# The third group of tokens joins the groups that are worked in seven products of halves

## The chip, the cores and the metric

The kernel runs on one core of a Trainium2 chip. Its engines are TensorE (PE, matrix products into PSUM banks), VectorE (DVE) and ScalarE (ACT), which work on SBUF and PSUM, GpSimd (POOL) and SyncE (SP), which here issues most transfers. Each engine takes its own instructions strictly in the order in which the program lists them, and waits at the first whose inputs or buffers are not ready. The metric is the device time of one execution in microseconds.

## The reference

```python
a = phi - np.max(phi, axis=2, keepdims=True)     # over the sequence
a = np.exp(a); a = a / (np.sum(a, axis=2, keepdims=True) + 1e-09)
k_m = np.einsum('bhsm,bhsd->bhmd', a, k)         # 32 memory slots per head
v_m = np.einsum('bhsm,bhsd->bhmd', a, v)
scores = 1.0 / np.sqrt(64) * np.matmul(q, k_m.transpose(0, 1, 3, 2))
attn = np.exp(scores - np.max(scores, axis=-1, keepdims=True))
attn = attn / (np.sum(attn, axis=-1, keepdims=True) + 1e-09)
x = np.matmul(attn, v_m).transpose(0, 2, 1, 3).reshape(4608, 512)
h = x @ w_in                                     # 512 x 2048
out = np.maximum(0.01 * h, h) @ w_out            # 2048 x 512
```

There are 8 batches of 576 tokens and 8 heads of 64 columns; all data are float32. Each batch's attention (steps a0 to a7) is followed by two dense products over all 4608 tokens.

## The kernel before

The heads' outputs are never formed. For each batch b the 256 rows of slot values are multiplied with w_in first, a "fold" in four quarters j (steps W{b}{j}): `.p` is the products on TensorE (L1241) into two PSUM banks `pa`, `.h0/.h1` ScalarE's high float16 halves of them (L1274), `.l0/.l1` VectorE's low halves (L1280). The pool of `pa` banks holds three, and the attention and the next fold use the same ones, so that a fold's products wait until the halves of the fold before have been taken. The folded quarter is then the weight of the first dense product, and the attention weights are its input. In float16 each product is three products: high by high, high by low, low by high.

The tokens are worked in groups. Groups 0 and 1 have 384 tokens (GT), group 2 had 256 (GL). These three go the old way: 8 units a group, each with two up-products (P, L1342, or u...P in the first group), the leaky step on ScalarE (V, L1349), a high half (C, L1361, ScalarE), a low half (L, L1365, VectorE) and the down-products (O, L1413) of 512 columns, for each 128 tokens and f tile three. The finished rows leave by Z (L1400).

The 4608 − 1024 other tokens are 14 late groups of 256 tokens and 512 inner columns at a time ("quarters", k = 4 per group). They go by seven products of halves in place of eight: up-products p (L1454), the leaky step v (L1468 and L1470), sums and differences of the four halves s (VectorE, L1484 to L1486), high halves c (ScalarE, L1490, 768 and 1024 columns), low halves l (VectorE, L1494, the same), and the seven down-products d (L1517), each 6 matmuls of 256 columns. Once for each group, x combines the results (L1527 on ScalarE, L1530 to L1537 on VectorE), and z scales and sends them (L1541). The very last group has steps of its own (end, L1564).

The order on all engines is written out by hand, as two lists of steps that run() calls in turn, OPENING (321 steps) and LATER (1846 steps): a step issues all its instructions, on whatever engines, at its place. The transfers stand in it too: i0 to i3 and o0 to o3 load and unpack the quarters of w_in and w_out (ld issues the transfers on SyncE, L389 and L393; y, t, h unpack them on VectorE and ScalarE, L405, L423, L403, L414; i3 is the last quarter of w_in). The slot sums of a batch are a{b}.C10 (L793), the reduction over its slots a{b}.A1 (L655), the transposing of scores L1119.

One SBUF tile, `arena`, holds what changes owner over time. The late groups' scratch lies where the loads and the old groups' halves lay before; `w_mem` holds batch 0's weights and then folded weights.

Of the kernel before, what the change touches and what calls it, by code (L numbers as in the profile page):

```python
# [52 lines left out]
a1.kv0 u3.V0 o2.h2 o2.h1 a1.A1 u2.O0 u3.V1 a1.A2 a1.A3 u4.P1 a1.B0 a1.kv2 a1.kv3 o2.t1 i1.b o2.y2
u4.P0 a1.B10 a1.B20 a1.B3 u3.O0 u4.V0 a1.C10 u5.P1 a1.C2 a1.q1 o2.t2 a1.q0 a1.C30 o0.b a1.C31 i3.ld1
u2.O1 a1.C4 i3.ld0 a1.Q1 o1.b a1.C3k i3.ld2 a1.D11 a1.D2 o2.b a1.D5 a1.D4 a1.D10 a1.D3 a1.Q0 i3.h0
u5.V1 u3.O1 o3.ld2 i3.h1 a1.E1 i3.y1 i2.b u4.V1 i3.t1 a1.E21 o3.ld1 i3.y2 i3.h2 i3.y0 i3.t2 a1.E20
i3.t0 u5.P0 u5.V0 u4.O0 o3.y2 o3.h2 i3.b u5.O0 a1.E22 f03.1 o3.t2 ci.1 o3.y1 a0.S18 u4.O1 a1.S01
a1.S11 ci.2 o3.h1 o3.ld0 a1.S02 a1.S03 ci.3 a1.S12 a1.S04 o3.t1 o3.y0 a2.phi f03.2 ci.4 o3.h0 e.
# [37 lines left out]
a3.D4 v2.2 Z2.1 W23.l0 p3.1 a3.Q1 a3.D5 a3.D6 d0.5 a4.A3 v3.1 d0.4 s2 p3.0 p3.3 c2.0 a4.B10 a3.E1
l2.0 v3.3 v3.0 d0.6 a3.E21 a3.E22 c2.1 p3.2 d1.2 d2.0 l2.1 p4.1 W30.p a4.B20 v3.2 d1.1 W30.h0 d1.4
v4.1 d2.2 p4.3 a3.E20 p4.0 s3 c3.0 W30.h1 l3.0 a3.E23 d1.6 c3.1 a4.kv d1.3 v4.0 W30.l0 p4.2 d2.1
v4.3 a3.S01 l3.1 W31.p d2.3 p5.1 W31.h0 d3.0 v4.2 a3.S02 v5.1 W31.h1 d2.4 os3 a4.B3 d1.5 p5.0 a3.S03
# [1631 lines left out]
```

## Time and profile before

| | us |
|---|---|
| runs | 640.47, 639.00, 640.07 (median 640.07) |
| the profiled execution | 639.66 |
| its span, first to last instruction | 637.9 |
| TensorE busy | 629.6 |
| VectorE busy | 518.1 |
| ScalarE busy | 402.0 |
| GpSimd busy | 12.5 |

The span is what the trace covers; 1.76 us of the execution lie around it. Busy times of matmuls are modelled and overlap in the lists, so that the sum over matmuls is more than the time they take up; spacings between their starts are not. The clock granted to TensorE was 0.999 of full speed over the run. All rows of the trace on which the prediction rests stand in a section of their own below.

### The profile page before, as it was taken

What the parts mean: (1) busy time and instruction counts of PE and PEld (TensorE: products, weight loads), DVE (VectorE), ACT (ScalarE), POOL (GpSimd) and SP (SyncE); (2) the same over time, 40 slices, a digit from 0 to 9 for tenths busy, and PEclk for the clock granted to TensorE, in tenths of its full rate; (3) what the DMA queues carried; (4) which work ended last, traced back from release to release, by engine and by line L of the source; (5) the groups of instructions that cost most, each with busy time, mean ns of one, the idle gap of its engine ahead of it and who ended that gap; (6) DMA issues with size and microseconds to landing.
All of it is one profiled execution on the core that took longest, in us unless ns stands there. A gap on an engine that the chain in (4) does not pass through costs nothing.

```text
span 637.9 us, 17249 instructions
## 1 busy us (share of the span) xinstructions
PE 629.6 (99%) x7365; PEld 490.0 (77%) x7365; DVE 518.1 (81%) x825; ACT 402.0 (63%) x698; POOL 12.5 (2%) x34
## 2 busy tenths in 40 slices
PE   8999999999999999999999999999999999999997
PEld 4545446666577788888888888888888989898886
DVE  5776799999889998898977788899788787755573
ACT  3898998967746665574555655655555656554560
POOL 0000120100000000000000000000000000000000
PEclk9999999999999999999999999999999999999999
DMA  9999821362334434414300504305041100010021
GB/s 326 351 392 271 274 83 25 102 113 75 117 74 83 166 54 95 150 42 65 84 10 17 165 19 93 72 10 183 2 76 35 35 1 17 19 34 2 4 61 37
DMA packets 85404, 61.16 MB, mean 96 GB/s; under 512 B 61648, under 2 KB 68560, under 8 KB 85328
## 3 DMA queue, kind: packets, MB, share of 16 engines
q1 hardware_dynamic: 84752, 59.51, 33.1%
q8 instruction: 58, 0.95, 0.6%
q10 hardware_dynamic: 576, 0.56, 0.3%
q14 instruction: 18, 0.15, 0.1%
HBM read 50.59 MB, written 9.45 MB: 94 GB/s over the span
## 4 chain that ended last, share of the span: by engine, by line
PE 90%; DMA 4%; DVE 3%; SPq 2%; issue 1%; ACT 1%; DVEq 0%
PE po L1517 32%; PE ph L1454 22%; PE po L1413 14%; PE ph L1342 7%; PE ph L1517 6%; PE pa L1241 4%; PE pa L793 2%; DMA arena<-in_moe_w_in_dram 2%; SPq L620 2%; DMA arena<-in_q_dram 1%; PE pa L1043 1%; DMA wo<-in_k_dram 1%; DVE arena L1494 1%; DVE r1k L655 0%; PE pa L1087 0%
## 5 line engine op out<-in xcount | busy, mean ns | idle before, releaser
L1517 PEld LDWEIGHTS <-arena 128*128 128x128 f16 x2352 | 226.8, 98 | 33.0 <-issue 7.8
L1454 PE MATMUL ph<-a,w_mem 128*128 128x256 f16 (+3 forms) x1512 | 146.8, 245 | 0.0
L1517 PE MATMUL po<-wo,arena 128*128 128x256 f16 x1008 | 130.3, 273 | 0.0
L1454 PEld LDWEIGHTS <-w_mem 128*128 128x128 f16 x1512 | 119.0, 98 | 13.6 <-issue 4.0
L1517 PE MATMUL po<-arena 128*128 128x256 f16 x1008 | 128.7, 273 | 0.0
L1468 ACT ACTIVATE wi<-ph,g_scs 128x256 f32<-128x256 f32 x112 | 52.8, 472 | 84.4 <-PE ph L1454 80.6
L1413 PE MATMUL po<-wo,arena 128*128 128x512 f16 (+1 forms) x336 | 99.4, 442 | 0.0
L1470 ACT ACTIVATE wi<-ph,g_scs 128x256 f32<-128x256 f32 x112 | 52.8, 471 | 67.4 <-PE ph L1454 59.9
L1494 DVE TENSOR_TENSOR arena<-arena 128x1024 f16<-128x1024 f32 x56 | 68.2, 1217 | 20.7 <-ACT arena L1490 20.6
L1494 DVE TENSOR_TENSOR arena<-wi,arena 128x768 f16<-128x768 f32 x56 | 53.3, 952 | 25.5 <-ACT arena L1490 25.2
L1490 ACT CAST arena<-arena 128x1024 f16<-128x1024 f32 x56 | 58.4, 1043 | 12.9 <-DVE arena L1486 11.9
L1342 PE MATMUL ph<-a,w_mem 128*128 128x192 f16 (+2 forms) x376 | 48.0, 278 | 0.0
L1490 ACT CAST arena<-wi 128x768 f16<-128x768 f32 x56 | 46.5, 830 | 2.3 <-PE po L1517 1.8
L1517 PE MATMUL ph<-wo,arena 128*128 128x256 f16 x336 | 45.7, 273 | 0.5 <-DVE t L1119 0.5
L1484 DVE TENSOR_TENSOR arena<-wi 128x512 f32<-128x512 f32 x56 | 38.2, 683 | 5.9 <-ACT wi L1468 4.3
L1413 PEld LDWEIGHTS <-arena 128*128 128x128 f16 x240 | 22.3, 98 | 25.4 <-issue 1.9
L1413 PEld LDWEIGHTS po<-wo,arena 128*128 128x128 f32 x96 | 17.5, 190 | 20.2 <-issue 18.1
L1280 DVE SCALAR_TENSOR_TENSOR w_mem<-pa,w_mem 128x512 f16<-128x512 f32 x40 | 26.4, 678 | 5.3 <-ACT w_mem L1274 5.3
L1241 PE MATMUL pa<-wi,vT 64*32 64x512 f16 (+1 forms) x704 | 28.9, 420 | 0.0
L1274 ACT ACTIVATE w_mem<-pa 128x512 f16<-128x512 f32 x40 | 22.8, 596 | 9.3 <-PE pa L1241 6.5
L1342 PEld LDWEIGHTS <-w_mem 128*128 128x128 f16 x312 | 23.1, 98 | 5.7 <-issue 2.8
L1486 DVE TENSOR_TENSOR arena<-wi,arena 128x256 f32<-128x256 f32 x56 | 23.8, 425 | 1.9
(238 smaller groups left out, 767.0 us busy)
## 6 DMA issues: line engine op xcount, KB each, us to landing
out_dram<-obs SPq DMA_DIRECT2D x138, 64.0 KB, 1.7
arena<-in_q_dram SPq DMA_DIRECT2D x96, 72.0 KB, 2.9
arena<-in_moe_w_in_dram SPq DMA_DIRECT2D x12, 512.0 KB, 6.7
arena<-in_moe_w_out_dram SPq DMA_DIRECT2D x8, 768.0 KB, 7.0
arena<-in_k_dram SPq DMA_DIRECT2D x5, 1152.0 KB, 5.9
arena<-in_v_dram SPq DMA_DIRECT2D x5, 1152.0 KB, 8.4
arena<-in_phi_dram SPq DMA_DIRECT2D x7, 576.0 KB, 4.9
arena<-in_k_dram SPq DMA_DIRECT2D x8, 288.0 KB, 4.9
```

The costliest lines, as they stand in the source:

```text
L1241: nc.tensor.matmul(pf[g][cols, :], lhs, rhs, start=(n == 0), stop=(n == len(passes) - 1), tile_position=(g * D, hh * M),)
L1280: nc.vector.scalar_tensor_tensor(tiles(t[:, 1]), w(g), ws, tiles(t[:, 0]), ALU.mult, ALU.subtract)
L1342: nc.tensor.matmul(ph[:, t0:t0 + n], lhs, rhs, start=(m == 0), stop=(m == len(seq) - 1))
L1413: nc.tensor.matmul(po, lhs, rhs, start=(f == 0 and m == 0), stop=(f == NQ * NF - 1 and m == len(seq) - 1),)
L1454: nc.tensor.matmul(ph[:, t0:t0 + n], lhs, rhs, start=(m == 0), stop=(m == len(seq) - 1))
L1468: nc.scalar.activation(dst, ph, AF.Prelu, scale=g_sc2n[:, j:j + 1], alpha=1.0 / SLOPE)
L1470: nc.scalar.activation(dst, ph, AF.Prelu, scale=g_sc2[:, j:j + 1], alpha=SLOPE)
L1484: nc.vector.tensor_tensor(gt[:, 0:2], two, gf[:, 1:3], ALU.subtract)
L1486: nc.vector.tensor_tensor(gt[:, 3], gf[:, 3], gt[:, 2], ALU.subtract)
L1490: nc.scalar.copy(dst[:, 0], src)
L1494: nc.vector.tensor_tensor(dst[:, 1], src, dst[:, 0], ALU.subtract)
L1517: nc.tensor.matmul(acc, g[:, x, s, u], rhs, start=(h == 0 and j == 0 and u == 0 and m == 0), stop=(j == NQ - 1 and u == 1 and m == 2), ski ...
```

## The change

Tokens 768 to 1023 become a late group: there are two old groups and 15 late ones, and k counts to 59. Old units 16 to 23 go. As the old buffers are still in use when the new group starts, its four quarters (k below 4) keep their values, sums and halves in other places: `w_mem` and a second place in the arena. A late group may now lie in batch 1, whose tokens are laid out in three blocks of 192, so that its up-products are split there. The scratch of the last quarter of w_out moves into `w_mem`, and the scores borrow a late group's bank by the batch's number (b > FB, from batch 3 on) instead of by whether the bank is already there.

```diff
-    G2 = 3
-    GL = 2 * P
-    X0 = 2 * S - P
+    G2 = 2
+    X0 = G2 * GT
+    GF_ODD = 64000
...
-            if j == NQ - 1 and x > 0:
-                t = obs[:, (x - 1) * E:x * E]
+            if j == NQ - 1:
+                t = obs[:, (x - 1) * E:x * E] if x else w_mem[:, E:2 * E]
...
-                if banks:
+                if b > FB:
                     psc.append(banks["p1"][:, EH:])
...
-        for b, tb, c0, t0, n in spans(G * GT, width(G)):
+        for b, tb, c0, t0, n in spans(G * GT, GT):
...
-            n = min(x1, (x // S + 1) * S) - x
+            m = SB if x < FB * S else S
+            n = min(x1, (x // m + 1) * m) - x
...
-            st["gf"] = wi[NQ][:, k % 2 * 1024:(k % 2 + 1) * 1024]
-            st["g"] = at(TMP + k % 3 * 7168, 7168).bitcast(F16)
+            if k < NQ:
+                st["gf"] = at(GF_ODD, 4096) if k % 2 else w_mem[:, 4 * 1024:]
+                st["gt"], slot = w_mem[:, 0:1024], k % 2
+            else:
+                st["gf"] = wi[NQ][:, k % 2 * 1024:(k % 2 + 1) * 1024]
+                st["gt"], slot = at(TMP + 3 * 7168, 4096), (k + 1) % 3
+            st["g"] = at(TMP + slot * 7168, 7168).bitcast(F16)
...
-        gt = at(TMP + 3 * 7168, 4096).rearrange("p (s x) -> p s x", s=4)
+        gt = st["gt"].rearrange("p (s x) -> p s x", s=4)
...
-W32.l1 d6.6 W32.l0 v9.1 d6.3 a5.kv c8.0 d7.0 p9.3 v9.3 a4.D2 a5.A1 v9.0 d6.5 a4.D11 s8 d7.2 c8.1
+a4.E21 p13.1 d9.6 d10.4 a4.D2 v13.1 a4.E22 a5.A1 v12.2 W32.p p13.3 W32.h0 p13.0 l11.1 d10.6 W32.h1
```

The lists of steps are the same for the first 110 steps and new from there on (321 and 1867 steps). A step of quarter k before is a step of quarter k + 4 now, as one group came ahead. Line numbers shift by a few: L1494 is now L1498, L1484 to L1486 are L1488 to L1490, L1280 is L1281, L655 is L656, L1119 is L1120.

VectorE where group 2's halves are made, a little behind the unpacking of the last quarter of w_in. L1365 is an old low half, L1280 a fold's low half, L464 a part of the sums of w_out's halves, L744 and L1172 belong to the attention of batches 2 and 3. Before:

```order
L1172 STREAM_TRANSPOSE t_1985<-t_1634 128x1152
L438 SCALAR_TENSOR_TENSOR wi_87<-wi_88,sw,wi_87 128x512
L723 TENSOR_TENSOR arena<-arena,r1k 128x1152
L1365 TENSOR_TENSOR arena<-arena 128x512
L438 SCALAR_TENSOR_TENSOR wi_88<-wi_89,sw,wi_88 128x512
L1206 TENSOR_TENSOR a<-t_1985,a 128x2x512
L1206 TENSOR_TENSOR a<-t_1985,a 128x2x64
L438 SCALAR_TENSOR_TENSOR wi_88<-wi_89,sw,wi_88 128x768
L1280 SCALAR_TENSOR_TENSOR w_mem<-pa,w_mem 128x512 x2
L464 SCALAR_TENSOR_TENSOR arena<-arena,sw 128x512
L744 TENSOR_REDUCE r1k<-arena 128x128
```

And now, at the same transposition of the same batch:

```order
L1173 STREAM_TRANSPOSE t_2005<-t_1653 128x1152
L1488 TENSOR_TENSOR w_mem<-w_mem 128x512
L1489 TENSOR_TENSOR w_mem<-w_mem 128x256
L1490 TENSOR_TENSOR w_mem<-w_mem 128x256
L439 SCALAR_TENSOR_TENSOR wi_88<-wi_89,sw,wi_88 128x768
L1281 SCALAR_TENSOR_TENSOR w_mem<-pa,w_mem 128x512
L1207 TENSOR_TENSOR a<-t_2005,a 128x2x512
L1207 TENSOR_TENSOR a<-t_2005,a 128x2x64
L1281 SCALAR_TENSOR_TENSOR w_mem<-pa,w_mem 128x512
L439 SCALAR_TENSOR_TENSOR wi_88<-wi_89,sw,wi_88 128x768
L745 TENSOR_REDUCE r1k<-arena 128x128
L1498 TENSOR_TENSOR arena<-w_mem,arena 128x1024
```

In place of one old low half the sums of a quarter (three instructions) and a low half of 1024 columns stand between the same steps of the attention and the folds.

VectorE ahead of the fold of batch 3's last quarter (W33.p, whose products come on TensorE as soon as the low halves L1280 of the quarter before have freed the banks). Before:

```order
L1494 TENSOR_TENSOR arena<-arena 128x1024
L1484 TENSOR_TENSOR arena<-wi_89 128x512
L1485 TENSOR_TENSOR arena<-wi_89,arena 128x256
L1486 TENSOR_TENSOR arena<-wi_89,arena 128x256
L1119 STREAM_TRANSPOSE t_3308<-pa 128x64
L1119 STREAM_TRANSPOSE t_3308<-pa 128x512 x2
L1494 TENSOR_TENSOR arena<-arena 128x1024
L1494 TENSOR_TENSOR arena<-wi_89,arena 128x768
L1280 SCALAR_TENSOR_TENSOR w_mem<-pa,w_mem 128x512 x2
L655 TENSOR_REDUCE r1k<-arena 128x128
```

And now:

```order
L1498 TENSOR_TENSOR arena<-wi_89,arena 128x768
L1291 TENSOR_SCALAR scales<-pv,pp_max 128x1
L1296 COPY scales<-scales 64x1
L1120 STREAM_TRANSPOSE t_3323<-pa 128x512
L1120 STREAM_TRANSPOSE t_3323<-pa 128x64
L656 TENSOR_REDUCE r1k<-arena 128x128
L1498 TENSOR_TENSOR arena<-arena 128x1024
L1488 TENSOR_TENSOR arena<-wi_89 128x512
L1489 TENSOR_TENSOR arena<-wi_89,arena 128x256
L1490 TENSOR_TENSOR arena<-wi_89,arena 128x256
L1281 SCALAR_TENSOR_TENSOR w_mem<-pa,w_mem 128x512 x2
```

The reduction of the next batch's slots (L655, now L656) stands ahead of the fold's two low halves instead of behind them, and so do the sums of a quarter.

## Rows read from the trace of the kernel before

**Rows 1.** The page: each engine's busy time and share; VectorE's 40 slices.

```profile
PE 629.6 (99%) x7365; PEld 490.0 (77%) x7365; DVE 518.1 (81%) x825; ACT 402.0 (63%) x698; POOL 12.5 (2%) x34
...
DVE  5776799999889998898977788899788787755573
```

**Rows 2.** Busy time of each engine by stretch of the span, instructions in brackets.

```profile
core 0: us, PE busy (x) PEld busy (x) DVE busy (x) ACT busy (x) POOL busy (x), PEclk, DMA share, GB/s
69.40:88.00 18.60, 18.60 (x107) 8.16 (x91) 16.18 (x35) 16.78 (x27) 3.63 (x3) 1.00 0.40 137
88.00:152.00 64.00, 64.00 (x629) 39.09 (x629) 63.09 (x105) 53.09 (x87) 4.37 (x7) 1.00 0.32 80
152.00:255.70 103.70, 103.70 (x1467) 78.60 (x1465) 95.23 (x151) 63.06 (x117) 0.20 (x2) 1.00 0.42 102
255.70:637.90 382.20, 377.73 (x4549) 330.00 (x4546) 296.86 (x454) 215.78 (x383) 0.10 (x1) 1.00 0.21 51
0.00:69.40 69.40, 65.53 (x639) 34.17 (x647) 46.73 (x84) 53.30 (x87) 4.21 (x21) 1.00 0.96 334
0.00:255.70 255.70, 251.83 (x2819) 160.02 (x2820) 221.23 (x372) 186.23 (x315) 12.41 (x33) 1.00 0.54 162
```

**Rows 3.** The chain of waits: start, duration, what ran, count.

```profile
142.72 3.88 PE po L1413 x18
...
156.90 0.11 PE pa L914
157.01 1.34 PE ph L1342 x24
...
324.43 2.62 PE po L1517 x24
```

**Rows 4.** Timeline of TensorE: start, duration, line, count, idle before.

```profile
57.90 2.48 PE L793 MATMUL pa<-arena 64*32 64x128 f32 x144
...
262.00 0.84 PE L1241 MATMUL pa<-wi,vT 64*32 64x512 f16 x24
...
322.31 0.81 PE L1517 MATMUL ph<-wo,arena 128*128 128x256 f16 x6 [0.48 <-DVE t L1119]
```

**Rows 5.** Groups by line and shape: total busy, mean ns, idle before.

```profile
L1517 PEld LDWEIGHTS <-arena 128*128 128x128 f16 x2352 | 226.8, 98 | 33.0 <-issue 7.8
...
L1494 DVE TENSOR_TENSOR arena<-arena 128x1024 f16<-128x1024 f32 x56 | 68.2, 1217 | 20.7 <-ACT arena L1490 20.6
...
L1494 DVE TENSOR_TENSOR arena<-wi,arena 128x768 f16<-128x768 f32 x56 | 53.3, 952 | 25.5 <-ACT arena L1490 25.2
...
L1484 DVE TENSOR_TENSOR arena<-wi 128x512 f32<-128x512 f32 x56 | 38.2, 683 | 5.9 <-ACT wi L1468 4.3 <-ACT wi L1470 0.6
L1280 DVE SCALAR_TENSOR_TENSOR w_mem<-pa,w_mem 128x512 f16<-128x512 f32 x40 | 26.4, 678 | 5.3 <-ACT w_mem L1274 5.3
...
L1486 DVE TENSOR_TENSOR arena<-wi,arena 128x256 f32<-128x256 f32 x56 | 23.8, 425 | 1.9
...
L655 DVE TENSOR_REDUCE r1k<-arena 128x128 f32<-128x1152 f32 x7 | 15.1, 2152 | 0.0
...
L1535 DVE TENSOR_TENSOR obs<-obs,po 128x512 f32<-128x512 f32 x13 | 8.9, 684 | 0.3
...
L1365 DVE TENSOR_TENSOR arena<-arena 128x512 f16<-128x512 f32 x8 | 5.4, 679 | 0.0
```

**Rows 6.** Timeline of VectorE.

```profile
69.42 1.03 DVE L405 TENSOR_SCALAR arena<-arena 128x768 uint32<-128x768 uint32 x2 [1.45 <-DMA arena<-in_moe_w_in_dram]
70.56 0.96 DVE L423 SCALAR_TENSOR_TENSOR wi<-arena 128x768 uint32<-128x768 uint32 x1
...
252.37 1.22 DVE L1494 TENSOR_TENSOR arena<-arena 128x1024 f16<-128x1024 f32 x1 [1.37 <-ACT arena L1490]
...
254.38 1.28 DVE L1280 SCALAR_TENSOR_TENSOR w_mem<-pa,w_mem 128x512 f16<-128x512 f32 x2
```

**Rows 7.** Timeline of SyncE's DMA queue.

```profile
60.23 2.82 SPq L393 DMA_DIRECT2D arena<-in_moe_w_in_dram  x5
```

More of the change, by code (lines that the diff above doesn't have):

```diff
@@ L53 @@
[L53 to L58, printed above, removed]
@@ L96 @@
[L96 to L99, printed above, removed]
-s4 p5.3 v5.0 d3.2 d2.5 p5.2 c4.1 W31.l0 W31.l1 a3.S04 c4.0 d2.6 v5.3 v5.2 x3.p a4.C10 p6.0 l4.1 l4.0
@@ new lines @@
+d8.5 p11.1 a4.C30 p11.0 d9.0 a4.C31 l9.1 v11.0 a3.S08 v11.1 a4.Q0 c10.0 x3.3 d9.1 s10 l10.0 a4.C3k
+d8.2 p11.2 d9.5 v11.2 d8.6 p12.0 p11.3 z3.0 a4.Q1 a4.D10 d8.3 a5.phi c10.1 v11.3 a4.D3 d9.2 p12.1
+l10.1 s11 v12.1 a4.E1 d10.5 a4.C4 os2 a4.E20 v12.0 p12.3 d8.4 c11.0 d9.4 v12.3 p12.2 l11.0 os3 c11.1
+a4.E21 p13.1 d9.6 d10.4 a4.D2 v13.1 a4.E22 a5.A1 v12.2 W32.p p13.3 W32.h0 p13.0 l11.1 d10.6 W32.h1
+s12 d11.6 c12.0 d10.2 d9.3 W32.l1 W32.l0 v13.3 v13.0 W33.p p13.2 d10.0 a4.D4 d10.1 d11.0 z3.1 d11.2
@@ new lines @@
+a4.D11 c12.1 v13.2 d11.1 a5.A2 l12.1 a4.D5 p14.1 p14.0 l12.0 s13 d10.3 W33.h1 c13.0 a4.E23 v14.0
+a5.A4 a5.kv v14.1 W33.l1 d11.3 d11.5 x4.p W33.h0 a4.D6 p14.3 p14.2 x4.0 c13.1 W40.p d11.4 v14.2
+l13.0 l13.1 v14.3 W33.l0 W40.h1 c14.0 d12.0 d12.5 p15.1 s14 c14.1 x4.1 a5.A3 x4.2 p15.0 d12.6 v15.1
+d12.3 x4.3 W40.l1 W40.h0 p15.3 l14.1 v15.0 d12.1 d13.1 p15.2 z4.0 os4 v15.2 v15.3 a5.B10 c15.0
+a5.B20 d12.2 d13.5 a4.S01 d13.2 p16.1 l14.0 W41.p d13.0 d12.4 v16.1 l15.0 p16.0 d14.0 a4.S02 v16.0
+z4.1 a4.S03 d14.2 p16.3 p16.2 d13.6 s15 W41.h0 a4.S04 d13.3 v16.2 d14.1 v16.3 p17.1 c15.1 W40.l0
@@ L184 @@
+z15.1 l58.0 c58.1 p59.2 v59.2 l58.1 d57.0 d57.6 v59.3 c59.0 d57.4 s59 d58.3 c59.1 z15.0 d58.4 d58.6
+l59.0 d58.0 d59.0 end.p l59.1 d58.2 d57.5 d59.2 d59.3 d59.6 d59.4 d58.5 d59.5 end.0 end.1 d57.1
+d58.1 end.2 end.3 end.z1 d59.1 end.4 end.z2 end.5 end.z0
 """
@@ L1303, in fold_scales @@
             )
-    def width(G):
-        return GL if G == G2 - 1 else GT
     def spans(x, n):
@@ L1354, in gf_old @@
     def gf_old(G, u):
-        n = 8 * width(G)
+        n = 8 * GT
         return at(G_OLD + (4 + u % 2) * 3072, n).rearrange("p (i x) -> p i x", i=2)
     def hi_old(G, u):
-        g = at(G_OLD + u % NGB * 3072, 8 * width(G)).bitcast(F16)
+        g = at(G_OLD + u % NGB * 3072, 8 * GT).bitcast(F16)
         g = gs[G, u] = g.rearrange("p (i f x) -> p i f x", i=2, f=2)
@@ L1419, in down @@
         if (u, i) == (0, 0):
-            pos[G] = [ps_o.tile([P, E], F32, name="po") for t in range(width(G) // P)]
-        for t in range(width(G) // P):
+            pos[G] = [ps_o.tile([P, E], F32, name="po") for t in range(GT // P)]
+        for t in range(GT // P):
             down_products(G, u, i, t)
@@ L1656, in unit @@
             steps[f"P{m}.{i}"] = lambda i=i: products(i)
-            steps[f"V{m}.{i}"] = lambda i=i: leaky(gf_old(G, u)[:, i], ph[i][:, 0:width(G)], G, u)
+            steps[f"V{m}.{i}"] = lambda i=i: leaky(gf_old(G, u)[:, i], ph[i][:, 0:GT], G, u)
             steps[f"O{m}.{i}"] = lambda i=i: down(G, u, i)
@@ L1664 @@
     for G in range(G2):
-        for t in range(width(G) // P):
+        for t in range(GT // P):
             steps[f"Z{G}.{t}"] = lambda G=G, t=t: store(G, t, pos[G][t])
```

225 lines of the change are left out of this document (112 added, 113 removed).

## The prediction, made before the changed kernel ran

> **What bounds the kernel now.** I read the page's shares and slices first [rows 1]. TensorE (PE) is busy 99% of the span, VectorE (DVE) 81%; the reader should see that VectorE's slices are full, 8 and 9 tenths, through the first half and loosen only behind it. The table by stretches says it in microseconds [rows 2]: from 88 to 152 us VectorE works 63.09 of 64 us and TensorE 64.00 of 64, both without a gap; from 152 to 255.7 VectorE works 95.23 of 103.7; from 255.7 on 296.86 of 382.2. So before 255.7 two engines are at their limit, and behind it only TensorE, with 85 us of room on VectorE.
>
> TensorE's busy time is modelled, so I took its pace from the chain of waits [rows 3]: 18 products of 512 columns take 3.88 us (215.6 ns each), 24 of 256 columns 2.62 us (109.2 ns), 24 of the mixed up-products 1.34 us (55.8 ns). The chain runs through TensorE's products one behind the other: the matmul stream sets the end as long as nothing makes TensorE wait. The list of its instructions does show one wait, 0.48 us ahead of the product at 322.31 [rows 4], far behind the part that changes. The granted clock is 1.00 in every stretch of rows 2.
>
> **The change part by part.**
>
> TensorE. Two halves' products instead of eight whole ones: tokens 768 to 1023 needed 16 f tiles x 2 token tiles x 3 = 96 down-products of 512 columns; now 4 quarters x 7 x 6 = 168 of 256 columns. That is −96 x 215.6 ns = −20.70 us and +168 x 109.2 ns = +18.35 us, together **−2.35 us**. The up-products of these tokens, 192 of mixed width, stay as they were. Their order is not the same, and that decides how the gain arrives, as follows.
>
> VectorE. The old way's eight low halves (679 ns each) go; each of the four quarters now needs the sums of halves (683 + 425 + 425 ns) and two low halves (1217 + 952 ns), 3.702 us, and the group three combining steps of 684 ns and one of 256 columns (425, as L1486) [rows 5]: 14.81 + 2.47 − 5.43 = **+11.85 us** on the engine that has no room before 255.7. Where? The order shows all of it, and a little more, ahead of the fold of batch 3's last quarter (W33.p), which before starts on TensorE at 262.00 [rows 4]. It needs the product banks that VectorE frees by the low half of the fold of the quarter before it (W32.l); before, these two low halves run at 254.38 and end at 255.66 [rows 6].
>
> What VectorE must have done before it frees them, after against before: four low halves of 1217 more (+4.87), four of 952 more (+3.81), the sums of five quarters more (5 x 683 + 10 x 425 = +7.67; four of the new group and one drawn ahead), the combine (+2.47), the reduction of the next batch's slots, moved from just behind these low halves to just ahead of them (L655, 2.152: +2.15), less eight old low halves (−5.43), less one of the two fold halves (−0.68, as the first one already frees a bank): +14.85. Neighbours overlap by some hundredths each; I take 0.2 off: +14.7. Before, VectorE worked 221.23 us of the first 255.7 [rows 2]. So after it must have worked **235.9 us**, and the fold starts no earlier than 235.9 us plus all the time that VectorE has idled until then.
>
> TensorE's own work before W33.p becomes less: −96 of 512 (−20.70), +144 of 256 (+15.72), 24 up-products moved behind it (−1.34), one transposing product of batch 4 less (−0.11, as at 156.90 [rows 3]): −6.4 us. On its own it would reach W33.p at 262.0 − 6.4 = 255.6. Behind W33.p it gets +24 of 256 (2.62), the 24 up-products (1.34) and the transposing product (0.11): +4.05 (rounded so that with the −6.4 it is the −2.35 again). So the −2.35 is a loan of −6.4 now and +4.05 later, and the early part can only be kept if VectorE has idled no more than 255.6 − 235.9 = 19.7 us by then. The change of the whole time is (idle − 19.7) − 2.35 = **idle − 22.05 us**, for idle above 19.7.
>
> VectorE's idle time. Before, it was 69.4 − 46.73 = 22.67 us by 69.4, then 2.42 by 88, 0.91 by 152 and 8.47 by 255.7 [rows 2], 34.5 in all. Of the first part little can go: at 69.42 VectorE begins to unpack the last quarter of w_in, after a wait for its transfer [rows 6]; SyncE issues that at 60.23 [rows 7], behind the slot sums of batch 1 at 57.90 [rows 4], and ahead of these sums TensorE has exactly the same products before and after. Only one of the two steps of that pair (half of 1.03 us) and one like the next row's (0.96) [rows 6] now come ahead of the piece that waits: VectorE has 48.1 us of work until that point, so at least 69.4 − 48.1 = **21.3 us** idle. That is one end. The other end is that it idles behind 69.4 as before, 2.42 + 0.91 + 8.47: 33.1 us. Between them I go by the row nearest to the new state. VectorE is now late at every step, as from 88 to 152, where it idled 0.91 us of 64; at that rate the 173 us from 88 to 261 cost 2.4. Of the 2.42 between 69.4 and 88, where it still catches up with transfers, I keep half, 1.2. The sum is 21.3 + 1.2 + 2.4 = **24.9 us**, W33.p at 235.9 + 24.9 = 260.8, and a change of 24.9 − 22.05 = **+2.85 us**.
>
> ScalarE casts the high halves of the new quarters too; it worked 63.06 us of 103.7 from 152 to 255.7 [rows 2], so this lies beside other work. If that cover were gone, the low halves would wait for it, as one does 1.37 us at 252.37 [rows 6]; that is inside the upper end of the idle time. The stores, the new places of the buffers and the splitting of the up-products at 192 columns add no instruction. Behind W33.p VectorE has 85 us to spare, so nothing is earned back or lost there: TensorE's work from there on is the same plus 4.05.
>
> A rule that speaks on TensorE's part: in rows 1 and 5 the weight loads are busy 490.0 us, 77% of the span, at 98 ns each. The Trainium skill, Perfetto Trace Analysis, section "Identifying the Most-Contended Engine", says that matmul busy time says little about how near TensorE is to its limit and that MFU and the busy share of weight loads should be used. By that, TensorE at 77% would come behind VectorE at 81%, and fewer products would be worth nothing: the last of the rivals below. The trace speaks against it: 24 products at 109.2 ns and 24 at 55.8 ns follow one another without a gap [rows 3], and TensorE is never without one in 88 to 255.7 [rows 2].
>
> Sum: 639.66 (the profiled execution) + 2.85 = **642.5 us**. That execution lies 0.41 below the median of the runs, 640.07; differences of under 0.2% (1.3 us) can't be told from no change, so the bounds are 638.8 and 641.35.
>
> **The rivals.**
>
> VectorE loses almost no time behind 69.4, as in the stretch from 88 to 152 all along: idle 21.3 to 23.3, a change of −0.75 to +1.25, about 640.3. For it: the 0.91 in 64 us. Against: the order puts waits for ScalarE's casts and for products in front of each low half (1.37 us for one [rows 6]), and before there were 8.47 us of them.
>
> TensorE's gain arrives whole: the last quarter of w_in lands 2 us earlier or more of VectorE's work fits ahead of it, so that idle stays below 20.8. Then 639.66 − 2.35 = 637.3 us. For it: the 22.67 us that VectorE stands idle in the first 69.4. Against: the sums at 57.90 that release the transfer stand behind the same products.
>
> The two full engines hold each other up: TensorE waits at a product for a low half, the next up-products come late, ScalarE and then VectorE wait for them. VectorE then idles as before, 33.1 us, and the change is +11.05: 650.7 us. It decides where the waits come before both engines have work queued, in 152 to 255.7; for it speaks the 8.47 there, against it that VectorE has 14.7 us more work queued than then.
>
> TensorE is limited by something beside the stream of columns, so that fewer of them are worth nothing: W33.p comes at 260.8 instead of 255.6, 24.9 − 19.7 = +5.2, 644.9 us. Against it stand the spacings of rows 3.
>
> **How the numbers follow.** The forecast (idle 23.3 to 29, 641 to 646.6) 0.50; almost no idle behind 69.4, 0.25; the gain whole, 0.14; the engines hold each other up, 0.10; weight loads, 0.01. Faster is the third, 0.14; the same the second, 0.25; slower the rest, 0.61. The range reaches down into the gain and up between forecast and the coupled case: 637.8 to 648.0. The likeliest case's own range is 641 to 646.6.
>
> **What would show it.** In the changed kernel VectorE must be busy over 97% from 88 to about 255 us and have idled 21 to 29 us when W33.p starts; W33.p near 260.8 and behind a wait of TensorE for VectorE (its low halves or the fold's), of some 5 us in all between 88 and 261. From W33.p to the end about 4 us longer than before, without new waits. If TensorE waits less than a microsecond and W33.p starts near 255.6, or if VectorE has idled under 21 us by then, the bound on the transfer is wrong, and so is the forecast; if TensorE waits over 10 us, the coupling is the right picture.

## The result, and the profile after

The changed kernel took 647.43 us (median of five runs, 646.36 to 648.5), the kernel before 640.07 in the same series: 1.0113 times as long, with a 95% interval of 1.0094 to 1.0132, that is +7.4 us. The forecast was 642.5 with a range of 637.8 to 648.0. The direction was right and the time lies at the upper edge of the range, above the 641 to 646.6 of the likeliest case; the change is two and a half times the forecast one. Of the six executions each of two kernels below (GpSimd's low halves, the low halves twice) one stood far out, at 1641.24 and 809.7 us, and is left out of their medians.

In the page of the profiled execution (647.43, span 645.6) VectorE's slices are full, 8 or 9 tenths, from the sixth to the twentieth; before, see [rows 1].

```profile
PE 630.3 (98%) x7437; PEld 496.7 (77%) x7437; DVE 529.7 (82%) x841; ACT 402.9 (62%) x699; POOL 14.3 (2%) x34
...
DVE  5866899999999999889969687978997977656564
```

VectorE works 11.6 us more than before (529.7 against 518.1; +11.85 was worked out), with 16 instructions more. The table of stretches answers to [rows 2]:

```profile
core 0: us, PE busy (x) PEld busy (x) DVE busy (x) ACT busy (x) POOL busy (x), PEclk, DMA share, GB/s
69.40:88.00 18.60, 18.00 (x165) 8.51 (x166) 16.83 (x36) 16.60 (x26) 5.07 (x5) 1.00 0.62 194
88.00:152.00 64.00, 62.92 (x627) 38.76 (x626) 63.07 (x100) 53.07 (x89) 5.79 (x7) 1.00 0.29 66
152.00:263.29 111.29, 108.77 (x1569) 88.38 (x1568) 108.51 (x172) 68.59 (x124) 0.20 (x2) 1.00 0.37 94
263.29:645.60 382.31, 376.55 (x4522) 328.36 (x4521) 293.42 (x451) 211.79 (x379) 0.10 (x1) 1.00 0.21 52
0.00:69.40 69.40, 64.10 (x557) 32.67 (x557) 47.86 (x86) 52.88 (x86) 3.14 (x19) 1.00 0.95 332
0.00:263.29 263.29, 253.80 (x2915) 168.32 (x2916) 236.28 (x391) 191.14 (x321) 14.20 (x33) 1.00 0.52 157
```

VectorE again works all but 0.93 us from 88 to 152, as before. By 69.4 it has idled 21.54 us (the floor in the prediction was 21.3), by 263.29 it has worked 236.28 us (235.9 was forecast) and idled 27.0 (24.9). There the fold W33.p stands:

```profile
257.90 0.84 PE L1242 MATMUL pa<-wi,vT 64*32 64x512 f16 x24
...
263.29 0.37 PE L1242 MATMUL pa<-wi,vT 64*32 64x512 f16 x1 [0.48 <-DVE w_mem L1281]
263.89 0.84 PE L1242 MATMUL pa<-wi,vT 64*32 64x512 f16 x23 [0.23 <-DVE w_mem L1281]
```

Before, it started at 262.00 [rows 4]; 260.8 was forecast. Now its first product comes at 263.29 and the others at 263.89, both behind a wait for the low halves of the fold before (L1281). The reader should note the two rows of one step: it takes two banks, and waits for each. The longest of TensorE's waits from 26 us on (engine, line, for what; us in all, times, longest) are these. With three more of 0.2 to 0.3 they make 6.7 us; the same list of the kernel before has two, 0.5 [rows 4] and 0.2 us:

```profile
PE ph L1453 <- ACT wi L1472: 1.2, 3, 0.5
PE pa L507 <- DVE diag L501: 1.1, 1, 1.1
PE po L1411 <- DVE wo L424: 0.8, 1, 0.8
PE pa L1088 <- ACT kT L937: 0.7, 1, 0.7
PE pa L1242 <- DVE w_mem L1281: 0.7, 2, 0.5
PE po L1521 <- DVE arena L1498: 0.6, 2, 0.3
PE po L1521 <- DVE obs L1539: 0.4, 1, 0.4
PE ph L1521 <- DVE arena L1498: 0.4, 1, 0.4
```

The products themselves run at the old spacing. In the chain, 18 products of 256 columns take 1.97 us (109.4 ns each; 109.2 in [rows 3]):

```profile
321.67 1.97 PE po L1521 x18
```

By the spacing a wait is longer than the list has it, as the list counts from a product's modelled end. Between these two rows stand twelve products, 1.31 us; TensorE lost 0.61 us, and the list gives 0.42:

```profile
239.19 1.50 PE L1521 MATMUL po<-wo,arena 128*128 128x256 f16 x12
241.11 0.83 PE L1521 MATMUL po<-wo,arena 128*128 128x256 f16 x6 [0.42 <-DVE obs L1539]
```

To see where all the time went I therefore compared each product's start with the sum of the spacings of all products ahead of it (each form's spacing as in the trace of before), from 25.8 us on. What is left is an estimate of the time that TensorE has lost until then, in us:

| until | 70 | 100 | 150 | 200 | 230 | 270 | 340 | end |
|---|---|---|---|---|---|---|---|---|
| before | 1.2 | 2.7 | 3.4 | 3.6 | 3.8 | 3.9 | 4.5 | 3.7 |
| after | 3.1 | 5.6 | 6.4 | 9.1 | 9.8 | 12.2 | 12.4 | 13.7 |
| no lows | 2.6 | 5.3 | 6.0 | 6.8 | 6.7 | 9.1 | 9.2 | 9.6 |
| lows twice | 2.8 | 5.4 | 6.2 | 13.4 | 14.3 | 16.8 | 16.6 | 17.5 |
| GpSimd's lows | 3.0 | 8.6 | 9.2 | 13.7 | 14.6 | 17.1 | 16.9 | 18.3 |
| fold first | 3.4 | 8.6 | 9.7 | 12.5 | 13.2 | 14.5 | 14.3 | 15.5 |
| slots later | 3.4 | 5.2 | 6.3 | 9.4 | 10.1 | 12.5 | 12.4 | 12.8 |
| three moves | 3.1 | 4.9 | 6.2 | 8.9 | 9.6 | 10.9 | 11.1 | 11.0 |
| old opening | 1.3 | 2.9 | 4.3 | 7.2 | 7.8 | 9.0 | 9.2 | 9.1 |
| five moves | 2.8 | 4.6 | 5.9 | 8.7 | 9.4 | 10.5 | 10.7 | 10.9 |
| five, no lows | 2.8 | 4.3 | 5.6 | 6.6 | 6.4 | 7.7 | 7.8 | 7.9 |
| five, no lows, no sums | 2.8 | 4.2 | 5.5 | 6.4 | 6.2 | 7.5 | 7.6 | 7.5 |
| before, lows thrice | 1.3 | 3.0 | 3.7 | 12.0 | 13.6 | 13.9 | 13.9 | 13.4 |
| before, late lows twice | 2.1 | 3.8 | 4.5 | 4.7 | 4.7 | 4.7 | 6.3 | 6.6 |

After minus before is 10.0 us at the end, and all products' spacings add up to 2.4 us less: 7.6, where the spans differ by 7.7. So the gain on TensorE is there, and 10.0 us of new losses with it: 2.9 by 100 us, 0.1 to 150, 2.5 to 200, 0.5 to 230, 2.3 to 270, and 1.7 behind it. The other rows belong to the experiments that follow; in none of them does TensorE make up more than 0.8 us of what it has lost.

### The profile page after: what moved, and what is told of

Its sections match the earlier page's. It is cut to its first block, busy times and chain, and to the rows that moved or that the text cites. A ratio compares the mean times of both kernels' runs of the same rounds, so it can differ in the third digit from the quotient of the medians.

```text
span 645.6 us, 17428 instructions
## 1 busy us (share of the span) xinstructions
PE 630.3 (98%) x7437; PEld 496.7 (77%) x7437; DVE 529.7 (82%) x841; ACT 402.9 (62%) x699; POOL 14.3 (2%) x34
## 4 chain that ended last, share of the span: by engine, by line
PE 52%; DVE 6%; SPq 3%; issue 1%; ACT 1%; DMA 0%; DVEq 0%; ACTq 0%
PE po L1521 27%; PE ph L1453 17%; PE ph L1521 4%; SPq L621 3%; PE pa L1242 2%; DVE arena L1498 1%; DVE arena L986 1%; PE pa L794 1%; DVE r1k L656 1%; PE pa L1044 1%; DVE arena L1488 1%; SPq L1394 0%; DMA arena<-in_q_dram 0%; DVE arena L1489 0%; DVE t L1120 0%
## 5 line engine op out<-in xcount | busy, mean ns | idle before, releaser
L1453 PE MATMUL ph<-a,w_mem 128*128 128x256 f16 (+3 forms) x1656 | 157.0, 243 | 1.0 <-ACT wi L1472 0.7
L1521 PE MATMUL po<-wo,arena 128*128 128x256 f16 x1080 | 139.6, 273 | 1.0 <-DVE arena L1498 0.6
L1521 PE MATMUL po<-arena 128*128 128x256 f16 x1080 | 140.0, 273 | 0.0
L1453 PEld LDWEIGHTS <-w_mem 128*128 128x128 f16 x1656 | 128.6, 98 | 14.8 <-issue 4.6
L1498 DVE TENSOR_TENSOR arena<-arena 128x1024 f16<-128x1024 f32 (+1 forms) x58 | 69.9, 1205 | 28.2 <-ACT arena L1494 28.2
L1411 PE MATMUL po<-wo,arena 128*128 128x512 f16 (+1 forms) x240 | 77.1, 467 | 0.8 <-DVE wo L424 0.8
L1494 ACT CAST arena<-arena 128x1024 f16<-128x1024 f32 (+1 forms) x58 | 60.2, 1037 | 21.8 <-DVE arena L1490 17.7
L1498 DVE TENSOR_TENSOR arena<-wi,arena 128x768 f16<-128x768 f32 x56 | 52.9, 948 | 6.0 <-ACT arena L1494 5.9
L1494 ACT CAST arena<-wi 128x768 f16<-128x768 f32 x56 | 46.6, 831 | 3.4 <-PE po L1521 2.9
L1488 DVE TENSOR_TENSOR arena<-wi 128x512 f32<-128x512 f32 x56 | 38.5, 687 | 8.5 <-ACT wi L1472 4.3
L1340 PE MATMUL ph<-a,w_mem 128*128 128x192 f16 (+1 forms) x232 | 38.0, 313 | 0.0
L1281 DVE SCALAR_TENSOR_TENSOR w_mem<-pa,w_mem 128x512 f16<-128x512 f32 x40 | 26.9, 681 | 7.0 <-ACT w_mem L1275 7.0
L1490 DVE TENSOR_TENSOR arena<-wi,arena 128x256 f32<-128x256 f32 x56 | 23.8, 425 | 2.0
L1453 PE MATMUL ph<-a,arena 128*128 128x256 f16 (+3 forms) x216 | 24.9, 237 | 0.5 <-ACT wi L1472 0.5
L1489 DVE TENSOR_TENSOR arena<-wi,arena 128x256 f32<-128x256 f32 x56 | 23.8, 425 | 1.9
```

Source lines behind the costliest of these rows:

```text
L1281: nc.vector.scalar_tensor_tensor(tiles(t[:, 1]), w(g), ws, tiles(t[:, 0]), ALU.mult, ALU.subtract)
L1340: nc.tensor.matmul(ph[:, t0:t0 + n], lhs, rhs, start=(m == 0), stop=(m == len(seq) - 1))
L1411: nc.tensor.matmul(po, lhs, rhs, start=(f == 0 and m == 0), stop=(f == NQ * NF - 1 and m == len(seq) - 1),)
L1453: nc.tensor.matmul(ph[:, t0:t0 + n], lhs, rhs, start=(m == 0), stop=(m == len(seq) - 1))
L1488: nc.vector.tensor_tensor(gt[:, 0:2], two, gf[:, 1:3], ALU.subtract)
L1489: nc.vector.tensor_tensor(gt[:, 2], gf[:, 1], gt[:, 1], ALU.subtract)
```

## The experiments

Each kernel is the changed one with one edit, unless it says "before"; times are medians, ratios (with their 95% intervals) are to the kernel before run beside it. That one's median differs a little from series to series: 640.1 beside the first four runs, 639.5 beside the slots later, the three moves, the old opening, the lows thrice and the late lows, 639.8 beside the five moves and the two kernels made from them. A diff of the lists of steps shows the steps around the moved ones alone. In what was expected, theory 1 or "amount" is the prediction's picture: the sum of VectorE's work ahead of W33.p decides. Theory 2 or "place" is: single waits, each where the new order has put a product close behind a late result.

**No low halves for the new group.** Their steps return without an instruction, and the down-products read the high half twice.

```diff
     def lo_g(k, h):
+        if k < NQ:
+            return
...
-                    acc, g[:, x, s, u], rhs, start=(...)
+                    acc, g[:, x if k >= NQ else 0, s, u], rhs, start=(...)
```

> The changed kernel without the eight low halves of the new group's four quarters (VectorE: 4 x 1.217 + 4 x 0.952 = 8.68 us of work gone from the stretch 130 to 255 us); its down-products read the high halves in their place, so that TensorE's work is the same and these tokens' results are rougher. Theory 1 (VectorE's queue of work is the limit until the fold W33.p, at 263.3 to 263.9 us): W33.p comes earlier until TensorE's own pace limits it, 255.6 plus the 2.9 us that TensorE has already waited more than before by 100 us, so about 258.5: 5 us less, 642 to 643 us. Theory 2 (waits at single places of the new order, whatever the amount of VectorE's work): at most 2 us less, 645.5 to 647. Theory 3 (TensorE itself is slower with more and smaller products): no change, 647.4.

Measured: 644.3 us, ratio 1.0066 (1.0044 to 1.0087), 3.1 us less than the change. Between the theories. In the table the loss from 150 to 200 shrinks from 2.7 to 0.8: there VectorE's work was what TensorE waited for. But the 2.4 us from 230 to 270 stay, though VectorE has 8.68 us less to do and has now idled 31.7 us by 263. W33.p comes 3.1 us earlier, and its two waits are the same to the hundredth:

```profile
260.17 0.37 PE L1242 MATMUL pa<-wi,vT 64*32 64x512 f16 x1 [0.48 <-DVE w_mem L1281]
260.77 0.84 PE L1242 MATMUL pa<-wi,vT 64*32 64x512 f16 x23 [0.23 <-DVE w_mem L1281]
```

The amount of VectorE's work does not hold that place.

**The low halves twice**, the other way round.

```diff
+        for _ in range(2 if k < NQ and h else 1):
-        nc.vector.tensor_tensor(dst[:, 1], src, dst[:, 0], ALU.subtract)
+            nc.vector.tensor_tensor(dst[:, 1], src, dst[:, 0], ALU.subtract)
```

> The changed kernel with the low half of 1024 columns of the new group's four quarters computed twice, one behind the other (VectorE: 4 x 1.217 = 4.87 us more, no other engine). Theory 1: VectorE has no slack left ahead of W33.p (0.93 us idle from 88 to 152, 2.8 from 152 to 263), so nearly all of it shows: 4 to 5 us more, 651.5 to 652.5. Theory 2: 0 to 2 us more, 647.5 to 649.5. Theory 3: 647.4.

Measured: 651.5 us, ratio 1.0181 (1.0156 to 1.0206), 4.1 us more than the change for 4.87 of work. This lies in theory 1's band and 2.0 above theory 2's. From 150 to 200 VectorE has hardly any slack: most of what is added shows, and there (in the table 7.2 us lost instead of 2.7).

**GpSimd's low halves.**

```diff
+        eng = nc.gpsimd if k < NQ else nc.vector
-        nc.vector.tensor_tensor(dst[:, 1], src, dst[:, 0], ALU.subtract)
+        eng.tensor_tensor(dst[:, 1], src, dst[:, 0], ALU.subtract)
```

> The same eight low halves, computed by GpSimd in place of VectorE, nothing else changed. GpSimd took 0.919 us for 384 columns of such a subtraction before, so about 2.45 us for 1024 and 1.85 for 768, 17 us in all on an engine that is busy 2%. Theory 1: as without them, 642 to 644 us, unless the down-products wait for a low half that comes 1.2 us later. Theory 2: 646 to 649, as the same places wait for a slower engine. Theory 3: 647.4.

Measured: 649.22 us, ratio 1.0149 (1.0122 to 1.0175), 1.8 more than the change, though the intervals overlap. It is no gain in any case, and the page tells why: VectorE has eight instructions less than the change (833 against 841) and yet is busy longer (531.3 us against 529.7).

```profile
PE 633.4 (97%) x7437; PEld 497.5 (76%) x7437; DVE 531.3 (82%) x833; ACT 402.9 (62%) x699; POOL 29.8 (5%) x42
```

VectorE's rows that lie beside GpSimd's stretch (L439 and L1160 take 0.75 and 1.35 us elsewhere):

```profile
175.48 2.13 DVE L439 SCALAR_TENSOR_TENSOR wi<-wi,sw,wi 128x512 f16<-128x512 f32 x1
177.54 3.28 DVE L1160 TENSOR_TENSOR t<-t,ts__1897 128x1152 f32<-128x1152 f32 x1
```

and GpSimd's two low halves at that place:

```profile
175.27 4.33 POOL L1499 TENSOR_TENSOR arena<-w_mem,arena 128x768 f16<-128x768 f32 x2 [6.76 <-ACT arena L1494]
```

Added up over the seven instructions that GpSimd's low halves stretched, it is about 8.75 us, as much as was taken off VectorE. The Trainium skill, SBUF — State Buffer, section "Who interferes with whom", says that a VectorE instruction with two SBUF inputs contends with a GpSimd instruction that reads SBUF, and that the port pair they share is an exclusive lock. The trace agrees: 3.28 us is 1.35 plus most of GpSimd's second 2.2 (4.33 us for the two). Work moved to GpSimd here is not moved off VectorE, so that this run says nothing for or against theory 1. Behind 150 us this kernel lost 9.1 us (9.2 to 18.3 in the table), the change 7.3; what its profile lost more by 100 is the same as in the next run's, and is told in the last section.

**The fold first.**

```diff
-a4.E22 a5.A1 v12.2 W32.p p13.3 W32.h0 p13.0 l11.1 d10.6 W32.h1 s12 d11.6
+a4.E22 v12.2 W32.p p13.3 W32.h0 p13.0 l11.1 d10.6 W32.h1 d11.6
-W32.l1 W32.l0 v13.3 v13.0 W33.p p13.2
+W32.l1 W32.l0 v13.3 v13.0 W33.p s12 a5.A1 p13.2
```

> The changed kernel with two steps moved from ahead of the fold W33.p to just behind it: the sums of quarter 12 (VectorE 1.53 us) and the reduction of batch 5's slots (2.15 us); no work added or taken away. Theory 1, with W33.p as the place that decides: W33.p 3.7 us earlier and the end 2.5 to 3.7 earlier, 643.7 to 645. Theory 1 with the limit spread over all later places until 300 us (VectorE must do that work anyway): 0 to 1 us less, 646.4 to 647.4. Theory 2: no change, or a new wait, 647 to 649.

Measured: 645.49 us, ratio 1.0082 (1.0057 to 1.0108), about 2 us less than the change, though the intervals overlap; between theory 1's two bands, and below theory 2's. In the change, VectorE's queue ahead of W33.p held these:

```profile
257.63 2.17 DVE L656 TENSOR_REDUCE r1k<-arena 128x128 f32<-128x1152 f32 x1
259.72 1.20 DVE L1498 TENSOR_TENSOR arena<-arena 128x1024 f16<-128x1024 f32 x1
261.03 0.69 DVE L1488 TENSOR_TENSOR arena<-wi 128x512 f32<-128x512 f32 x1
...
262.56 1.28 DVE L1281 SCALAR_TENSOR_TENSOR w_mem<-pa,w_mem 128x512 f16<-128x512 f32 x2
```

while ScalarE had the fold's high halves ready at 259.89:

```profile
258.81 1.08 ACT L1275 ACTIVATE w_mem<-pa 128x512 f16<-128x512 f32 x2 [1.46 <-PE pa L1242]
```

The low halves, 1.28 us, came at 262.56, behind 2.17 us of the next batch's reduction, a low half and 1.53 us of sums. With the fold first VectorE waits for ScalarE instead and has them done in time,

```profile
263.29 1.29 DVE L1281 SCALAR_TENSOR_TENSOR w_mem<-pa,w_mem 128x512 f16<-128x512 f32 x2 [1.07 <-ACT w_mem L1275]
...
266.01 2.19 DVE L656 TENSOR_REDUCE r1k<-arena 128x128 f32<-128x1152 f32 x1
```

and TensorE runs from fold to fold (261.27, 266.10) without a wait:

```profile
261.27 0.84 PE L1242 MATMUL pa<-wi,vT 64*32 64x512 f16 x24
...
266.10 0.84 PE L1242 MATMUL pa<-wi,vT 64*32 64x512 f16 x24
```

From 260 to 270 it now loses 0.2 us (14.27 to 14.48) instead of 1.15 (11.06 to 12.21). But not 3.7: VectorE's work that was moved away did not carry W33.p forward by its length, as theory 1 wants. This profile is that of the slowest of the six executions (648.91) and also lost 3 us more by 100; see the last section.

**The slots later.** The new order has two steps of batch 2's attention (L692, L724) ahead of the bound of w_out (steps co), on which all later scales depend.

```diff
-W00.l1 co.1 a1.S07 W01.h0 a2.A3 a2.B10 co.2 u7.P1
+W00.l1 co.1 a1.S07 W01.h0 co.2 u7.P1
...
-i0.l1 co.4 W10.l0
+i0.l1 co.4 a2.A3 a2.B10 W10.l0
```

> The changed kernel with two steps of batch 2's attention (L692 and L724 on VectorE, 0.38 and 1.35 us when alone) moved from ahead of the bound of w_out's size to behind it, where the kernel before has them too; no work added or taken away. There TensorE waits 1.08 us at 92.81 in the changed kernel's trace, 1.98 us and some more behind it in those of the runs with the fold first and with GpSimd's low halves, where L692 and L724 stretch to 1.11 and 2.53 us beside GpSimd's instructions. Place theory: that wait goes for good, 1 to 3 us less, 644.5 to 646.4. Amount theory: VectorE has as much to do until W33.p, 647 to 648.

Measured: 646.29 us, ratio 1.0108 (1.0093 to 1.0123): 1.1 less, but only 0.5 less when each is counted from the kernel before run beside it, and not to be told from the change by its interval. The trace shows the wait of 1.08 us gone, and L692 and L724 at their usual length,

```profile
93.36 0.40 DVE L692 TENSOR_TENSOR r1k<-r1k 128x128 f32<-128x128 f32 x1
93.79 1.36 DVE L724 TENSOR_TENSOR arena<-arena,r1k 128x1152 f32<-128x1152 f32 x1
```

where in the change L724 and L501 lay beside GpSimd's L1160:

```profile
88.97 0.39 DVE L692 TENSOR_TENSOR r1k<-r1k 128x128 f32<-128x128 f32 x1
89.39 1.96 DVE L724 TENSOR_TENSOR arena<-arena,r1k 128x1152 f32<-128x1152 f32 x1
...
91.94 0.82 DVE L501 TENSOR_SCALAR diag<-ident,m 4x4 f32<-4x4 f32 x1
```

```profile
90.10 2.60 POOL L1160 TENSOR_TENSOR t<-t,ts__886 128x768 f32<-128x768 f32 x1
```

**Three moves**: both of these, and a third that turned out to shift one of ScalarE's casts past steps of other engines and so leaves every engine's order as it was.

```diff
-x3.0 d7.5 x3.1 c9.1 v10.3 v10.2 a3.S07 x3.2
+x3.0 d7.5 x3.1 c9.1 v10.3 v10.2 x3.2 a3.S07
```

> The changed kernel with three moves: the two steps of the run before, the two steps of the run with the fold first (645.5), and a transposition of batch 3 (L1173, 1.37 us) moved from ahead of the third combining step at 240.37 to behind it, for whose result TensorE waits 0.42 us at 241.11. No work added or taken away. Place theory: the gains add up, 2 for the fold, 1 to 3 for the slots, 0.5 for the combine: 641.5 to 644. Amount theory: as the fold first alone, 645 to 646.

Measured: 644.3 us, ratio 1.0081 (1.0064 to 1.0098), 0.3 above the place theory's band, and below the amount theory's. Counted from the kernel before run beside each, the gains add up (2.0 and 0.5; 2.5 together); the third wait stayed.

**The old opening** on top: the steps up to a1.C10 in the order before.

```diff
-i1.y0 i1.t0 u0.P1 u1.V0 a0.S11 o0.h0 o0.y0 o0.h1 o1.ld1 i1.h2 i2.ld1 a0.S12 o1.ld2 o0.t0 o0.y1 o0.t1
+o0.h0 u1.P1 o1.ld1 u1.V0 o0.y0 a0.S11 u0.P1 i1.y0 o0.t0 i2.ld1 o1.ld2 o0.y1 o0.h1 i1.h2 i1.y2 i1.y1
...
```

> The three moves, and the steps of the opening up to the slot sums of batch 1 (at 57.9 us) in the order that they have in the kernel before; what is left follows in the new order. In the changed kernel TensorE waits 0.81 us at 32.29 for an unpacked piece of w_out and has lost 1.9 us more than before by 70 us. Place theory: 0.9 to 1.9 less than the three moves alone, 640 to 643. Amount theory: VectorE has idled 22.7 us by 69.4 as before, not 21.5, so 1 us more than the three moves alone.

Measured: 643.67 us, ratio 1.0067 (1.0054 to 1.0081). Lower by 0.6 instead of 0.9 to 1.9, 0.7 above the band, and not clear of the three moves' interval. In its trace, which is that of the fastest of the five (642.6), TensorE has lost 1.3 by 70 us instead of 3.1 and the wait at 32.29 is gone; yet in the next three kernels, with the same opening, it is 2.8 again. The opening hangs on transfers and differs from one execution to another; how much of the change's 1.9 us by 70 is the order's stays open. VectorE's idle time by 69.4 was 21.0, not 22.7.

**Five moves**: the transposition itself (a3.S06) behind the combining step, and the leaky step v11.3 ahead of the cast c10.1.

```diff
-a5.phi c10.1 v11.3 a4.D3
+a5.phi v11.3 c10.1 a4.D3
```

> The kernel with the old opening (643.7 us) and two more moves: the transposition of batch 3 (L1173, 1.37 us) now really behind the third combining step (the move made for that before shifted a cast and left every engine's order as it was), and the leaky step whose bank TensorE awaits at 248.36 (0.47 us) from behind a cast of 1.05 us to ahead of it. No work added or taken away. Place theory: both waits go, 0.42 + 0.47 and what lies beside them, about 1 us less: 642.2 to 643.2. Amount theory: no change, 643.7.

Measured: 644.84 us, ratio 1.0073 (1.0058 to 1.0088). A miss: both waits went (0.42 and 0.47), and one of about their size came a little behind them, where the products of the next batch's slots wait for a transposition that now stands later:

```profile
250.64 0.25 PE L1044 MATMUL pa<-arena,x_k 64*32 64x64 f32 x2 [0.60 <-DVE arena L986]
```

From 70 us to the end it loses 8.1 us, the run before 7.8; that its time is 1.2 us longer comes for the most part from the opening.

**Five moves without the low halves**, and then **without the sums** too (with constants cast in place of the sums). The low halves go as in the first run; the sums go so:

```diff
     def add_g(k):
...
+        if k < NQ:
+            return
...
```

> The run with five moves without the eight low halves of the new group's four quarters (VectorE: 8.68 us less; TensorE reads the high halves in their place). Place theory: only what TensorE still waits for these halves and behind them from 150 to 200 us goes, 2 to 2.5 us (2.9 lost there more than before the change): 639.7 to 641 us. Amount theory: VectorE's 8.68 us show until TensorE's own pace limits: 637 to 638.5.

Measured: 641.61 us, ratio 1.0026 (1.0015 to 1.0037), 3.2 less than with them. Nearer to the place theory (0.6 above its band), far from the amount theory's 637 to 638.5.

> As the run before, and without the sums of the halves of these four quarters as well (VectorE: 4 x 1.53 = 6.1 us less, 14.8 in all; ScalarE casts constants of the same size instead; those tokens' results are wrong). With that the change costs VectorE less than nothing, and what is left is TensorE's part. If TensorE's -2.35 us are real and waits were all that hid them: 637.5 to 639.5. If fewer columns on TensorE are worth nothing (weight loads or another limit): 640.5 or more.

Measured: 641.08 us, ratio 1.0021 (1.0011 to 1.0031). By the number it falls to "worth nothing", but I had set the alternative wrongly. The table has 7.5 us lost in it against 3.7 before, 3.8 more, and 2.4 off for the products: +1.4, where the spans differ by 1.2 (639.1 and 637.9). So TensorE's gain is there, and waits of the new order that have nothing to do with the new group's work on VectorE still outweigh it. That all 14.8 us of that work were worth 3.8 us, and the last 6.1 of them 0.5, is the clearest count against my picture. Of the 3.8 us, 1.6 are lost by 70 us, ahead of all of the new group's work, and the other 2.2 by themselves would leave the gain almost even. No run has the change with its later steps in an order nearer to the old one, so that how much of the rest is the change's and how much this order's stays open.

**The kernel before with its third group's low halves thrice.**

```diff
+        for _ in range(3 if G == 2 else 1):
-        nc.vector.tensor_tensor(g[:, 1], gf_old(G, u), g[:, 0], ALU.subtract)
+            nc.vector.tensor_tensor(g[:, 1], gf_old(G, u), g[:, 0], ALU.subtract)
```

> The kernel before, with each of the eight low halves of its third group computed three times (VectorE: 16 x 0.679 = 10.86 us more between 155 and 192 us, about the 11.85 that the change adds; nothing else). Amount theory (only the sum of VectorE's work ahead of W33.p counts, which it awaits at 262.0 with 8.5 us of idle time behind 152 to use up): ready at 255.0 + 10.86 - 7 = 258.9, before TensorE comes: 640 to 641.5 us. Place theory (products that stand close behind a late piece of VectorE's wait at once, and what TensorE lost is not made up): 3 to 8 us more, 643 to 648.

Measured: 651.37 us, ratio 1.0187 (1.0167 to 1.0208): 11.9 us for 10.86 of work. The profile is that of the fastest of the five (649.23; the spans differ by 9.5 us); its granted clock was 0.997, that of the other four 0.995. Some 1.6 of the 9.5 are a fall of the clock (see the last section): 24 up-products take 1.99 us from start to start instead of 1.43, and 24 of 512 columns behind them 6.19 instead of 5.17. The 8.5 us that VectorE idled from 152 to 255.7 before were not used up: by 263 it has idled 33.4 us, before 35.4. TensorE waited close behind the added work, at once and for good:

```profile
166.03 2.17 PE L1342 MATMUL ph<-a,w_mem 128*128 128x192 f16 x24 [1.57 <-ACT arena L1349]
...
184.98 0.83 PE L1342 MATMUL ph<-a,w_mem 128*128 128x192 f16 x12 [0.58 <-ACT arena L1349]
...
187.93 0.45 PE L1455 MATMUL ph<-a,w_mem 128*128 128x128 f16 x5 [1.73 <-DVE w_mem L1280]
...
199.69 1.04 PE L1414 MATMUL po<-wo,arena 128*128 128x512 f16 x4 [0.87 <-DVE arena L1366]
...
204.34 0.84 PE L1241 MATMUL pa<-wi,vT 64*32 64x512 f16 x23 [0.67 <-DVE arena L1280]
```

Where it waited for ScalarE's leaky step (L1349), that step had itself waited for the added low halves:

```profile
165.51 0.84 ACT L1349 ACTIVATE arena<-ph,g_scs 128x256 f32<-128x256 f32 x2 [1.91 <-DVE arena L1366]
```

**The kernel before with nine late low halves twice**, spread over 309 to 560 us.

```diff
+        for _ in range(2 if h and k in range(14, 50, 4) else 1):
```

> The kernel before, with the low half of 1024 columns of nine late quarters (every fourth from the 14th to the 46th, 309 us to about 560) computed twice: 9 x 1.217 = 10.95 us more on VectorE, as much as the 10.86 between 155 and 192 us that cost 11.9 us, but where VectorE is busy 80 to 85% in every 50 us and TensorE waits for nothing. Place theory (VectorE's work costs where its queue is full and a product stands close behind it): 0 to 1.5 us more, 639.8 to 641.3. A plain sum of VectorE's work, wherever it lies: about 11 us more, 651.

Measured: 642.43 us, ratio 1.0043 (1.0027 to 1.0058): 2.9 us for 10.95 of work, a quarter of what the same work cost between 155 and 192, though 1.1 above the band. In its profile 1.1 of the 2.8 us by which the spans differ stand ahead of the first added instruction (the first of the folds L1241 behind 240 us starts at 253.2 instead of 252.1), so that the work's own share may be nearer to 1.7. Before, VectorE is busy 80 to 85% of the time there, and even so some of it shows.

No version here beats the kernel before.

## Why the prediction was right, and where it was not

The direction was right, and the time fell into the range because the range reached up towards the coupled case, not because the likeliest case's sum held.

The sum on TensorE: the spacings hold and −2.4 us are in the trace; no run shows them as a net gain. The weight loads play no part: 256 columns still take 109.4 ns.

The sum on VectorE: +11.6 us measured (+11.85), 236.28 us of work ahead of W33.p (235.9), 21.54 us idle by 69.4 (21.3; its own terms give 21.2). The last piece of w_in was issued at 61.02 behind the same slot sums at 58.79, as argued. (The second rival's 640.3 is counted from the median, 640.07; from 639.66, as the other sums are, its middle is 639.9.)

What is short is the sum "idle − 22.05", term by term. VectorE's idle time until W33.p was 27.0 us instead of 24.9: +2.1; its work +0.4. The fold's second bank came 0.6 later than its first, which the sum left out. Behind W33.p I had put "nothing is earned back or lost there"; the table has 1.5 us lost behind 270, where before it gives back 0.2: +1.7. 2.85 + 2.1 + 0.4 + 0.6 + 1.7 is 7.65, and the spans differ by 7.7. Of the signs set beforehand, VectorE's share (98.5% from 88 to 152, 97.5% from there to W33.p) and its idle time came; W33.p came 2.5 us late, and new waits stood behind it.

The step that failed is the one that made a rate out of it: that VectorE, being late at every step, would hardly idle, so that its work and idle time could be added up to one place. The books balance, but they are not the cause. Taking 8.68 us of VectorE's work away moved W33.p by 3.1 us, and VectorE had idled 4.5 us more by then. The likely picture is the rival that I gave 0.10, in a smaller form: TensorE and VectorE are both full, each keeps to its own order, and every product that stands too close behind a result costs its wait for good. As numbers its bands did badly: they were met once (the slots later), and missed by 3.4 us with the lows thrice and by 2.0 with the low halves twice, the one run that met the amount theory's band. But where the two theories lie far apart (the lows thrice, five moves without low halves, the late low halves) the amount theory was off by 9.9, 3.1 and 8.6 us, the place theory by 3.4, 0.6 and 1.1.

About 2 of the 10.0 us are VectorE's load from 150 to 200 (shown by the run without low halves), about 1 is the fold behind the reduction (from the trace of the fold first; the time alone is not clear of its interval), about 1 is the two slots steps (likewise). Even the three moves, with both of them, are not quite clear of the change: 1.0064 to 1.0098 against 1.0094 to 1.0132. The rest is open. At 240 to 250 the five moves took two waits away and others came. What the opening costs differs from execution to execution. Behind 340 the change loses 1.3 us, and 0.4 or less in seven of the ten kernels made from it, also in the slots later, whose edit stands 250 us ahead of that place; why is not shown.

## What to carry to other kernels

When one engine runs without a gap, its lost time only adds up. So price a new order wait by wait: for each product, what stands ahead of its input on the engine that makes it, and how many microseconds lie between the two in the engine's own queue; an engine's idle total says little about it. Here, work added where the other engine's queue is full cost most of its length or all (4.1 of 4.87 us; 11.9 of 10.86, falls of the clock included), and a quarter of it or less where that engine is busy 80 to 85% (2.9 of 10.95).
